# Layers' border of attention and two MLPs: last sums of two batches added by transfers and loaded back, products released before weight sums

## The chip, the core and the metric

The kernel runs on one core of one Trainium2 chip. What is measured is the device time of one execution in microseconds (us). PE is TensorE, which multiplies; DVE is VectorE, ACT is ScalarE, POOL is GpSimd; SP is SyncE, which here only issues transfers (DMAs). Each of these works through a queue of its own in order, and an instruction that waits holds up everything behind it on its queue.

## What is computed

Band attention with a few global rows gives 4 batches of 544 tokens with 512 features. They go through two MLPs ("layer 0" and "layer 1"), each with 2048 hidden columns, in float32:

```python
x = attn_out.transpose(0, 2, 1, 3).reshape(B * S, H * D)
h = x @ w_in
x = where(h > 0, h, exp(minimum(h, 0)) - 1) @ w_out         # layer 0
h = x @ w_in2
x = where(h >= 1, h, where(h <= -1, 0, (h + 1)**2 / 4)) @ w_out2   # layer 1
```

## The kernel before

A float32 number is held as two parts (high and low), and each product of two such numbers is three matmuls of 128 x 512 on PE. The 2048 hidden columns of a layer are 16 blocks `f` of 128. Two blocks make a "pair" `n`: pairs 0 to 5 are blocks 4 to 15 of layer 0, pairs 6 to 13 are all of layer 1. Four blocks, two pairs, are a "column group" `c`; two batches `j` make a "duo" (batches 0 and 1, batches 2 and 3).

**Up.** For a pair and a duo, `quad` makes eight outputs from seven products by a Strassen-like scheme: products of the weights themselves (A11, A12, A22) and of sums of weights (S1 to S4) with forms of the tokens (X11, X21, T1 and so on). `decode_in` loads a pair's raw weights into a tile named `wraw` (a pool of two tiles of 1 MB), DVE and ACT decode them into the tile `wi` (lines 213 to 239), then DVE makes the sums of weights (names `whole`, `mixed`, the last of them `wi<-mixed,wi`). `product` asks by `need` that the pair stands in `pairs_in`, which `decode_in` sets when the sums are made. `decode_out` loads and decodes the weights of the second matmul in the same way, into `wo`.

**Down.** `down` multiplies the hidden values with `wo`, over the four blocks of a column group, into four PSUM banks `dn`, one for each 128 features. `collect` takes a bank away: in most column groups ACT copies it to a tile `ev` (line 347) and a transfer issued by POOL adds it to a sum in HBM (line 352). In the last column group of a layer `so_far` holds the sum of the groups before, loaded in one transfer of 1 MB (lines 1153, 1156) while the group runs, and DVE adds the bank to it (line 355). For batches 0 and 1 that tile is one of the two `wraw` tiles; for batches 2 and 3 it is a tile `sums`.

**The border.** The layer-0 sums in `so_far` are the tokens of layer 1. `later_forms` makes their seven forms, on DVE (names `xl<-sum`, `sum<-sum`, `mixed`) and ACT (`xh<-sum`), and SP stores them for later column groups. It gets going when `summed[j]` says that the batch's last sums are issued, and it is done with a `wraw` tile only after the last form, when the next raw weights can be loaded into it.

What is written here is a program of jobs (`job_at`, `event`, `pop`): after each product a job may step and one `down` may go. From layer 0's second part on, the build's scheduler orders the instructions of each engine anew.

Of the kernel before, what the change touches and what calls it, by code (L numbers as in the profile page):

```python
# [9 lines left out]
F32 = mybir.dt.float32  # L10
# [11 lines left out]
B, H, SL, SG, D = 4, 8, 512, 32, 64  # L22
# [4 lines left out]
P = 128  # L27
# [4 lines left out]
KT = DM // P  # L32
NF = DFF // P
# [34 lines left out]
BLOCK = 2 * P  # L68
# [9 lines left out]
def band_attention_then_two_mlps(  # L78
# [40 lines left out]
    for j in range(B):  # L119
# [3 lines left out]
    so_far = {}  # L123
    dram = ctx.enter_context(tc.tile_pool(name="dram", bufs=1, space=bass.MemoryType.DRAM))

    sums = {
        (layer, j): dram.tile([P, KT, SL], F32, name=f"sum{layer}_{j}")
        for layer in range(3)
        for j in range(B)
    }  # L130
# [23 lines left out]
    eng = pinned  # L154
# [21 lines left out]
    def in_order(tag, ins):  # L176


        if eng is free:
            if tag in newest:  # L180
                tc.add_manual_dep(ins.ins, newest[tag].ins.name, IN_ORDER, reason="order of tiles")
            newest[tag] = ins

    w_in, w_out, rows_in = {}, {}, {}
# [14 lines left out]
    def decode(wtmp_p, raw, hi, lo):  # L199

        n = raw.shape[1]
        words = raw.bitcast(U32).rearrange("p (n two) -> p n two", two=2)
        low, high = words[:, :, 0], words[:, :, 1]
        top = wtmp_p.tile([P, n], U32, tag="top", name="top")
        if eng is pinned:
            power = wtmp_p.tile([P, n], U32, tag="power", name="power")
        else:
            power = raw.bitcast(U32)[:, 0:n]
        rest = wtmp_p.tile([P, n], U32, tag="rest", name="rest")
        yield  # L210

        if eng is free:
            in_order("top", eng.scalar.activation(top.bitcast(F32), high.bitcast(F32), AF.Abs))
        in_order(
            "rest",
            eng.vector.tensor_scalar(
                rest, high, 0x1FF, 15, ALU.bitwise_and, ALU.logical_shift_left
            ),
        )
        eng.vector.scalar_tensor_tensor(  # L220
            rest, low, 17, rest, ALU.logical_shift_right, ALU.bitwise_or
        )
        yield
        if eng is pinned:
            eng.scalar.activation(top.bitcast(F32), high.bitcast(F32), AF.Abs)
            yield

        eng.vector.tensor_scalar(
            top.bitcast(F32), top.bitcast(F32), SMALLEST, 1.0, ALU.max, ALU.mult
        )  # L230

        eng.vector.tensor_scalar(top, top, 3, 0x3FFFF000, ALU.logical_shift_left, ALU.bitwise_and)
        eng.vector.scalar_tensor_tensor(
            top, high, 0xC0000000, top, ALU.bitwise_and, ALU.bitwise_or
        )
        yield
        eng.scalar.activation(hi, top.bitcast(F32), AF.Copy)
        eng.vector.tensor_scalar(power, top, 0xFF800000, None, ALU.bitwise_and)
        eng.vector.scalar_tensor_tensor(
            lo, rest, 2.0 ** -35, power.bitcast(F32), ALU.mult, ALU.mult  # L240
        )
# [182 lines left out]
    def mpool(name, bufs, **kw):  # L424
        return ctx.enter_context(tc.tile_pool(name=name, bufs=bufs, reuse_waits="tile", **kw))
# [4 lines left out]
    with ExitStack() as actx:  # L430
# [413 lines left out]
        eng = free  # L844
# [5 lines left out]
    wraw_p = mpool("wraw", 2, side="right")  # L850
    wtmp_p = mpool("wtmp", 1, side="right")
    w_ps = [mpool("w_more", 1, side="right")]
# [1 line left out]
    ps_up.append(mpool("ps_up", 1, space=PSUM))  # L854
    ps_dn.append(mpool("ps_dn1", 1, space=PSUM))

    pairs_in, slot = {}, {}

    def add(out, a, b, op=ALU.add):

# [2 lines left out]
    def words(n, srcs):  # L863

        raw = wraw_p.tile([P, n * len(srcs)], U64, tag="wraw", name="wraw")
        for i, src in enumerate(srcs):
            ins = eng.sync.dma_start(raw[:, i * n:(i + 1) * n], src)
            if i == 0:
                in_order("wraw", ins)
        return raw  # L870
# [12 lines left out]
    def of_pair(n):  # L883

        layer, q = (0, n + 2) if n < 6 else (1, n - 6)
        return layer, (2 * q, 2 * q + 1)

    def decode_in(n):

        layer, fs = of_pair(n)  # L890
        raw = words(KT * P, [(w1, w2)[layer][f][:, 0:KT * P] for f in fs])
        yield
        w = w_ps[n % 3 // 2].tile([P, 2, 8 * BLOCK], F32R, tag=f"wi{n % 3}", name="wi")
        for _ in decode(wtmp_p, raw, w[:, 0, 0:4 * BLOCK], w[:, 1, 0:4 * BLOCK]):
            pass
        yield
        x = wtmp_p.tile([P, 4 * BLOCK], F32, tag="rest", name="whole")
        y = wtmp_p.tile([P, 4 * BLOCK], F32, tag="top", name="mixed")
        at = lambda t, c: t[:, c % (4 * BLOCK):c % (4 * BLOCK) + BLOCK]
        whole = add(  # L900
            x, w[:, 0, 0:4 * BLOCK].bitcast(F32), w[:, 1, 0:4 * BLOCK].bitcast(F32)
        )
        in_order("rest", whole)
        in_order("top", add(at(y, S1), at(x, A21), at(x, A22)))
        add(at(y, S2), at(y, S1), at(x, A11), ALU.subtract)
        add(at(y, S3), at(x, A11), at(x, A21), ALU.subtract)
        add(at(y, S4), at(x, A12), at(y, S2), ALU.subtract)
        hi = w[:, 0, 4 * BLOCK:]
        eng.scalar.activation(hi, y, AF.Copy)
        add(w[:, 1, 4 * BLOCK:], y, hi.bitcast(F32), ALU.subtract)  # L910
        pairs_in[n] = w
        rows_in[1, n] = lambda k, part: w[:, part, 0:4 * BLOCK].rearrange("p (f c) -> p f c", f=2)[
            :, :, k * P:(k + 1) * P
        ]

    def decode_out(n):

# [118 lines left out]
    made_forms, holds, summed, w_out_uses = set(), {}, {}, {}  # L1036
# [10 lines left out]

    def product(n, duo, col, i, then):

        need(lambda: n in pairs_in and holds.get(i) == (of_pair(n)[0], duo))  # L1050
        ps, w, x = up_bank(), pairs_in[n], slot[i]
        for k in range(2):
            for t, (a, b) in enumerate(((1, 0), (0, 1), (0, 0))):
                eng.tensor.matmul(  # L1054
                    ps,
                    w[:, a, col + k * P:col + (k + 1) * P],
                    x[b][:, k * SL:(k + 1) * SL],
                    start=k + t == 0,
                    stop=k == 1 and t == 2,
                )  # L1060
        if then is not None:

            if then + (i,) in made_forms:
                load_form(*then, i)
            else:
                holds[i] = "free"
        return ps
# [67 lines left out]
    def pop():  # L1135

        kind, *rest = downs.pop(0)
        if kind == "rows":
            _, u, layer, fs = rest
            down_rows(layer, fs, u)  # L1140
            if NF - 1 in fs:
                soon.setdefault(now[0] + 1, []).append(lambda: turn_rows(layer))
        else:
            layer, fs, j, f, ds = rest
            if f == fs[0] and len(ds) == KT:
                banks[j] = {}
            if f == fs[2 % len(fs)] and NF - 1 in fs:

                if layer == 0 and j >= 2:
                    if j == 2:  # L1150
                        spare.append(w_ps[1].tile([P, 2, 2 * BLOCK * 4], F32, tag="wi2", name="sums"))
                    so_far[layer, j] = spare[0][:, j % 2].rearrange("p (k n) -> p k n", k=KT)
                    eng.sync.dma_start(so_far[layer, j], sums[layer + 1, j])
                else:
                    so_far[layer, j] = wraw_p.tile([P, KT, SL], F32, tag="wraw", name="sum")
                    in_order("wraw", eng.sync.dma_start(so_far[layer, j], sums[layer + 1, j]))
            down(layer, fs, j, f, banks[j], ds)
            if f == fs[-1] and NF - 1 in fs and layer == 0:
                summed[j] = KT
        for f in fs if kind == "rows" else [f]:  # L1160
            if (layer, f) in pair_of:
                w_out_uses[pair_of[layer, f]] -= 1

    spare = []
    pair_of = {(of_pair(n)[0], f): n for n in range(14) for f in of_pair(n)[1]}
# [21 lines left out]
    def need(done):  # L1187

        tries = 0
        while not done():  # L1190
            step(line[0])
            tries += 1
            assert tries < 100, "what is needed is not under way"
# [26 lines left out]
    for i, js in enumerate(((0, 1, 2, 3), (2, 3, 0, 1))):  # L1220
        fs = PLAIN[i]
# [30 lines left out]
    for c in range(7):  # L1252
        at = base + 17 * c
        job_at(at + 1, decode_out(2 * c + 1))
        if c < 6:
            late = 3 if c == 3 else 0
            if c == 3:
                job_at(at + 2, later_forms(1), False)
            job_at(at + 5 + late, decode_in(2 * c + 2))
            job_at(at + 8 + late, decode_out(2 * c + 2))  # L1260
            if c == 2:
                job_at(at + 9, later_forms(0), False)
            job_at(at + 12 + late // 3, decode_in(2 * c + 3))
    for g, (c, duo) in enumerate(groups):
        n0, n1 = ns = (2 * c, 2 * c + 1)
        layer = of_pair(n0)[0]
        fs = [f for n in ns for f in of_pair(n)[1]]
# [86 lines left out]
```

## Time and profile before

| | us |
|---|---|
| median of 3 runs | 852.78 (851.49 to 853.75) |
| the profiled execution's own time | 852.66 |
| its span on the core | 850.9 |
| PE busy | 814.0 (96%) |
| DVE busy | 685.6 (81%) |
| ACT busy | 554.3 (65%) |
| POOL busy | 102.3 (12%) |

The span is the stretch from the first to the last instruction in the trace; the time has 1.8 us more around it. Matmuls overlap in the trace (one is shown with 0.39 us while they start 0.227 us apart), so PE's busy share says little; idle time in front of a matmul, and matmuls that start further apart, say more. The border of the two layers lies between 420 and 535 us.

### The profile page before, as it was taken

The page shows a single profiled execution, that of the slowest core. Times are in us where ns is not written, and L with a number is a line of the kernel's source. Part 1 is how long each engine was busy: PE and PEld are TensorE (multiplying, and loading weights), DVE is VectorE, ACT ScalarE, POOL GpSimd, SP SyncE. Part 2 cuts the span into 40 slices and gives each one's busy share as a digit, 9 for nine tenths or more (in the row PEclk, how much of TensorE's full clock was granted, in tenths as well). Part 3 has the DMA queues.
Part 4 walks back from the last instruction along what each step waited for, and adds up shares of the span by engine and source line. Part 5 has one row for each costly group of instructions (what it writes and reads, how often), then busy time and mean ns, then how long its engine had stood idle before and what let it go on. Part 6 is the DMA issues. An engine that isn't in the chain of part 4 may idle for free.

```text
span 850.9 us, 15914 instructions
## 1 busy us (share of the span) xinstructions
PE 814.0 (96%) x6058; PEld 662.6 (78%) x6058; DVE 685.6 (81%) x1279; ACT 554.3 (65%) x948; POOL 102.3 (12%) x162
## 2 busy tenths in 40 slices
PE   8799999998979999999999988999999999999998
PEld 5676778886758888888888866788888888888886
DVE  5798889968869979786789899998988598945463
ACT  5788765855746667555656366878867686867451
POOL 2231300002213022201100000000020111111000
PEclk9999999999999999999999999999999999999999
DMA  8988729997999189538916846437853795369523
GB/s 268 318 262 275 255 85 373 370 392 213 298 328 160 43 245 318 115 65 211 313 69 247 297 187 259 148 99 250 294 119 79 198 323 123 49 142 302 200 101 110
DMA packets 67132, 180.88 MB, mean 213 GB/s; under 512 B 9328, under 2 KB 9584, under 8 KB 65904
## 3 DMA queue, kind: packets, MB, share of 16 engines
q1 hardware_dynamic: 55248, 158.62, 53.8%
q0 software_dynamic: 11520, 20.98, 15.3%
q8 instruction: 48, 0.79, 0.4%
q10 hardware_dynamic: 288, 0.26, 0.1%
q14 instruction: 28, 0.23, 0.1%
HBM read 116.65 MB, written 63.18 MB: 211 GB/s over the span
## 4 chain that ended last, share of the span: by engine, by line
PE 76%; DMA 11%; DVE 7%; ACT 5%; issue 2%; POOL 0%; SPq 0%; ACTq 0%; DVEq 0%; POOLq 0%
PE dn L368 34%; PE up L1054 26%; DMA wraw<-in_w 5%; PE up L281 3%; PE dn L381 2%; DMA xh<-form 2%; PE s L146 2%; PE up L293 2%; DMA k_sb<-in_kT 1%; PE pt L146 1%; DMA sum<-ev 1%; PE up L146 1%; PE po L146 1%; ACT sn L146 1%; DVE xl L861 1%
## 5 line engine op out<-in xcount | busy, mean ns | idle before, releaser
L1054 PE MATMUL up<-xh,wi 128*128 128x512 f32 x784 | 264.5, 397 | 12.8 <-DMA xh<-form 3.9
L368 PE MATMUL dn<-gh,wo 128*128 128x512 f32 x608 | 184.6, 391 | 3.7 <-ACT ev L347 3.4
L1054 PEld LDWEIGHTS up<-xh,wi 128*128 128x128 f32 x784 | 149.9, 191 | 47.6 <-DVE u L861 4.9
L861 DVE TENSOR_TENSOR u<-up,u 128x512 f32<-128x512 f32 x196 | 131.7, 686 | 51.4 <-PE up L1054 43.2
L1054 PE MATMUL up<-xl,wi 128*128 128x512 f32 x392 | 155.0, 395 | 0.0
L352 POOL DMA_DIRECT2D sum<-ev x80 | 72.7, 1118 | 593.8 <-ACT ev L347 588.9
L368 PEld LDWEIGHTS dn<-gh,wo 128*128 128x128 f32 x608 | 113.5, 188 | 29.2 <-ACT ev L347 5.5
L368 PE MATMUL dn<-gl,wo 128*128 128x512 f32 x304 | 114.4, 390 | 0.4 <-DVE gl L334 0.4
L330 ACT ACTIVATE gh<-g 128x512 fp32r<-128x512 f32 x123 | 77.1, 628 | 53.1 <-DVE g L313 20.0
L334 DVE TENSOR_TENSOR gl<-g,gh 128x512 fp32r<-128x512 f32 x123 | 84.0, 686 | 13.0 <-ACT gh L330 11.8
L1054 PEld LDWEIGHTS up<-xl,wi 128*128 128x128 f32 x392 | 75.0, 191 | 14.9
L347 ACT ACTIVATE ev<-dn 128x512 f32<-128x512 f32 x110 | 61.7, 597 | 34.2 <-PE dn L368 19.6
L306 ACT ACTIVATE g<-u,half_sb 128x512 f32<-128x512 f32 x64 | 45.8, 720 | 48.2 <-DVE u L861 40.0
L368 PEld LDWEIGHTS dn<-gl,wo 128*128 128x128 f32 x304 | 57.0, 188 | 12.8 <-DVE gl L334 0.9
L368 PE MATMUL dn<-gh,xl 128*128 128x512 f32 x160 | 62.2, 392 | 2.6 <-ACT gh L330 2.5
L368 PE MATMUL dn<-gh,xh 128*128 128x512 f32 x160 | 62.3, 389 | 0.0
L315 DVE TENSOR_TENSOR g<-u,g 128x512 f32<-128x512 f32 x64 | 43.8, 686 | 20.9 <-ACT g L308 20.9
L368 PE MATMUL dn<-gl,xh 128*128 128x512 f32 x160 | 58.4, 389 | 0.0
L307 ACT ACTIVATE g<-g,one_sb 128x512 f32<-128x512 f32 x68 | 48.7, 720 | 1.4
L301 ACT ACTIVATE g<-u 128x512 f32<-128x512 f32 x48 | 30.1, 630 | 26.1 <-DVE u L861 22.4
L303 ACT ACTIVATE g<-g,one_sb 128x512 f32<-128x512 f32 (+1 forms) x64 | 45.6, 714 | 1.5
L308 ACT ACTIVATE g<-g 128x512 f32<-128x512 f32 x68 | 42.5, 627 | 1.1
(189 smaller groups left out, 1357.3 us busy)
## 6 DMA issues: line engine op xcount, KB each, us to landing
wraw<-in_w SPq DMA_DIRECT2D x56, 512.0 KB, 6.6
xh<-form SPq DMA_DIRECT2D x46, 512.0 KB, 9.6
xl<-form SPq DMA_DIRECT2D x46, 512.0 KB, 8.1
sum<-ev POOLq DMA_DIRECT2D x80, 256.0 KB, 8.4
v_sb<-in_vwin SPq DMA_DIRECT2D x64, 260.0 KB, 4.6
form<-xh SPq DMA_DIRECT2D x20, 512.0 KB, 4.6
form<-xl SPq DMA_DIRECT2D x20, 512.0 KB, 4.3
sum<-ev SPq DMA_DIRECT2D x32, 256.0 KB, 5.4
```

The lines of the kernel that those rows point to most:

```text
L146: return lambda *args, **kw: tc.keep_in_program_order(fn(*args, **kw))
L303: eng.scalar.activation(self.g, self.g, AF.Relu, bias=one_sb, scale=-1.0)
L306: eng.scalar.activation(self.g, self.ps, AF.Relu, bias=half_sb, scale=-0.5)
L307: eng.scalar.activation(self.g, self.g, AF.Relu, bias=one_sb, scale=-1.0)
L315: eng.vector.tensor_tensor(g, self.ps, g, ALU.max)
L330: eng.scalar.activation(self.gh, self.g, AF.Copy)
L334: eng.vector.tensor_tensor(self.gl, self.g, self.gh.bitcast(F32), ALU.subtract)
L347: eng.scalar.activation(out, ps, AF.Copy)
L352: eng.gpsimd.dma_start(to, out, accum_op=ALU.add)
L368: eng.tensor.matmul(banks[d], w[:, d * P:(d + 1) * P], g, start=first and k == 0, stop=last and k == 2)
L861: return eng.vector.tensor_tensor(out, a, b, op)
L1054: eng.tensor.matmul(ps, w[:, a, col + k * P:col + (k + 1) * P], x[b][:, k * SL:(k + 1) * SL], start=k + t == 0, stop=k == 1 and t == 2,)
```

## The change

1. In layer 0's last column group, batches 0 and 2 (the first of each duo) no longer add on DVE. Their `so_far` is not set while `down` runs, so `collect` copies each bank on ACT and adds it to the sum in HBM by a transfer of POOL's. When the batch's last `down` is issued, `all_so_far` loads the finished sum in one transfer, and `summed` is set.
2. `pairs_in[n]` is set as soon as a pair's weights are decoded; a new set `sums_in` is filled when the sums of weights are made. A product of the weights themselves asks for the first, a product of sums for the second.
3. In the first column group of layer 1 (c = 3), two of the weight jobs come one event later (`late` 4 for 3).

```diff
-    pairs_in, slot = {}, {}
+    pairs_in, sums_in, slot = {}, set(), {}
...
         for _ in decode(wtmp_p, raw, w[:, 0, 0:4 * BLOCK], w[:, 1, 0:4 * BLOCK]):
             pass
+        pairs_in[n] = w
+        rows_in[1, n] = lambda k, part: ...
         yield
...
         add(w[:, 1, 4 * BLOCK:], y, hi.bitcast(F32), ALU.subtract)
-        pairs_in[n] = w
-        rows_in[1, n] = lambda k, part: ...
+        sums_in.add(n)
...
-        need(lambda: n in pairs_in and holds.get(i) == (of_pair(n)[0], duo))
+        there = pairs_in if col < 4 * BLOCK else sums_in
+        need(lambda: n in there and holds.get(i) == (of_pair(n)[0], duo))
...
-            if f == fs[2 % len(fs)] and NF - 1 in fs:
-
-                if layer == 0 and j >= 2:
-                    if j == 2:
-                        spare.append(w_ps[1].tile([P, 2, 2 * BLOCK * 4], F32, tag="wi2", name="sums"))
-                    so_far[layer, j] = spare[0][:, j % 2].rearrange("p (k n) -> p k n", k=KT)
-                    eng.sync.dma_start(so_far[layer, j], sums[layer + 1, j])
-                else:
-                    so_far[layer, j] = wraw_p.tile([P, KT, SL], F32, tag="wraw", name="sum")
-                    in_order("wraw", eng.sync.dma_start(so_far[layer, j], sums[layer + 1, j]))
+            by_hand = NF - 1 in fs and (layer == 1 or j % 2)
+            if by_hand and f == fs[2 % len(fs)]:
+
+                all_so_far(layer, j)
             down(layer, fs, j, f, banks[j], ds)
             if f == fs[-1] and NF - 1 in fs and layer == 0:
+                if not by_hand:
+                    all_so_far(layer, j)
                 summed[j] = KT
...
-            late = 3 if c == 3 else 0
+            late = 4 if c == 3 else 0
```

`all_so_far` holds the removed lines as a function. The scheduler moves much around the border, of which three places matter below.

**SP's queue ahead of layer 1's first weights.** `sum1_0` and `sum1_1` are the sums of batches 0 and 1 in HBM, `wraw` from `in_w2` are raw weights of layer 1 (here those of `decode_out` for pair 6), `form0` are token forms. Before (the load of `sum1_0` stands six rows above these):

```order
L1027 DMA xh_5577<-form0_1_3_125 128x1024
L867 DMA wraw_5724<-in_w2 128x512 x2
L1027 DMA xl_5600<-form0_1_5_127 128x1024
L1027 DMA xh_5599<-form0_1_5_127 128x1024
L1027 DMA xl_5644<-form0_1_6_128 128x1024
L1027 DMA xh_5643<-form0_1_6_128 128x1024
L1156 DMA sum_5853<-sum1_1_108 128x2048
```

Now:

```order
L1028 DMA xl_5600<-form0_1_5_127 128x1024
L1028 DMA xh_5599<-form0_1_5_127 128x1024
L1028 DMA xl_5644<-form0_1_6_128 128x1024
L1028 DMA xh_5643<-form0_1_6_128 128x1024
L1171 DMA sum_5730<-sum1_0_107 128x2048
L867 DMA wraw_5732<-in_w2 128x512 x2
L1171 DMA sum_5861<-sum1_1_108 128x2048
```

The load of batch 0's sum has moved behind the last token forms, and the raw weights have moved behind it.

**DVE's queue in the last column group of layer 0.** `L216` begins the decoding of those raw weights, `L355` are adds of batch 0 and `u<-up` sums of products. Before:

```order
L861 TENSOR_TENSOR wi_5624<-mixed_5671,wi_5624 128x1024
L216 TENSOR_SCALAR rest_5780<-wraw_5724 128x1024
L334 TENSOR_TENSOR gl_5610<-g_5604,gh_5608 128x512
L313 SCALAR_TENSOR_TENSOR g_5648<-u_5393,g_5648 128x512
L220 SCALAR_TENSOR_TENSOR rest_5780<-wraw_5724,rest_5780 128x1024
L228 TENSOR_SCALAR top_5779<-top_5779 128x1024
L334 TENSOR_TENSOR gl_5654<-g_5648,gh_5652 128x512
L232 TENSOR_SCALAR top_5779<-top_5779 128x1024
L313 SCALAR_TENSOR_TENSOR g_5704<-up_5679,g_5704 128x512
L355 TENSOR_TENSOR sum_5656<-dn_5551,sum_5656 128x512
```

Now, ten rows after the same `wi<-mixed,wi`:

```order
L861 TENSOR_TENSOR u_5813<-up_5806,u_5742 128x512
L216 TENSOR_SCALAR rest_5788<-wraw_5732 128x1024
L861 TENSOR_TENSOR u_5834<-up_5827,u_5813 128x512
L220 SCALAR_TENSOR_TENSOR rest_5788<-wraw_5732,rest_5788 128x1024
L861 TENSOR_TENSOR u_5742<-up_5827,u_5742 128x512
L228 TENSOR_SCALAR top_5787<-top_5787 128x1024
L861 TENSOR_TENSOR u_5813<-up_5845,u_5813 128x512
L313 SCALAR_TENSOR_TENSOR g_5837<-u_5834,g_5837 128x512
L232 TENSOR_SCALAR top_5787<-top_5787 128x1024
L233 SCALAR_TENSOR_TENSOR top_5787<-wraw_5732,top_5787 128x1024
```

The decoding now begins ten instructions later, among the sums of products. The four adds of batch 0 are gone; those of batch 1 (`L355 sum_5861<-dn_5761` and three more) stand 22 instructions behind this `L216` row.

**ACT's queue at the first evictions of layer 1.** `ev<-dn` empties the banks of layer 1's first batch, `L237` makes the high part of decoded weights. Before:

```order
L306 ACTIVATE g_6521<-up_6496,half_sb_71 128x512
L308 ACTIVATE g_6469<-g_6469 128x512
L347 ACTIVATE ev_6529<-dn_6385 128x512
L347 ACTIVATE ev_6535<-dn_6389 128x512
L347 ACTIVATE ev_6541<-dn_6393 128x512
L307 ACTIVATE g_6521<-g_6521,one_sb_72 128x512
L347 ACTIVATE ev_6547<-dn_6397 128x512
L237 ACTIVATE wi_6605<-top_6606 128x1024
```

Now:

```order
L306 ACTIVATE g_6537<-up_6512,half_sb_71 128x512
L308 ACTIVATE g_6485<-g_6485 128x512
L307 ACTIVATE g_6537<-g_6537,one_sb_72 128x512
L237 ACTIVATE wi_6650<-top_6651 128x1024
L308 ACTIVATE g_6537<-g_6537 128x512
L347 ACTIVATE ev_6545<-dn_6401 128x512
L347 ACTIVATE ev_6551<-dn_6405 128x512
```

The evictions have moved behind the high part of the next pair's weights.

## Rows read from the trace of the kernel before

**Rows 1.** Windows: us, PE, PEld, DVE, ACT, POOL busy, PEclk, DMA share, GB/s.
```profile
483.00:535.00 52.00, 43.36 (x183) 33.94 (x182) 51.08 (x66) 33.40 (x49) 0.00 (x0) 0.93 0.58 215
535.00:560.00 25.00, 25.00 (x113) 20.67 (x113) 23.47 (x35) 19.92 (x31) 0.00 (x0) 1.00 0.49 152
...
500.00:505.00 5.00, 4.19 (x12) 3.26 (x13) 5.00 (x7) 1.91 (x3) 0.00 (x0) 0.68 0.27 107
```

**Rows 2.** Chain of waits that ended last, at 395 us: start, us, what.
```profile
395.15 2.72 PE up L1054 x12
```

**Rows 3.** Timeline of PE: start, us, instruction, in brackets idle before and releaser.
```profile
422.34 1.55 PE L368 MATMUL dn<-gh,wo 128*128 128x512 f32 x6
424.33 0.97 PE L368 MATMUL dn<-gl,wo 128*128 128x512 f32 x3 [0.44 <-DVE gl L334]
...
425.82 0.40 PE L1054 MATMUL up<-xh,wi 128*128 128x512 f32 x1
...
496.21 0.50 PE L1054 MATMUL up<-xh,wi 128*128 128x512 f32 x1 [0.83 <-DVE u L861]
...
500.81 0.50 PE L1054 MATMUL up<-xh,wi 128*128 128x512 f32 x1 [2.95 <-DVE wi L861]
...
514.23 0.50 PE L1054 MATMUL up<-xh,wi 128*128 128x512 f32 x1 [1.80 <-DVE u L861]
...
529.45 0.50 PE L368 MATMUL dn<-gh,xl 128*128 128x512 f32 x1 [1.98 <-ACT gh L330]
...
533.09 0.73 PE L368 MATMUL dn<-gh,wo 128*128 128x512 f32 x2 [0.63 <-ACT ev L347]
```

**Rows 4.** Timeline of DVE, 422 to 530 us, same columns.
```profile
422.98 0.69 DVE L216 TENSOR_SCALAR rest<-wraw 128x1024 uint32<-128x1024 uint32 x1 [3.61 <-DMA wraw<-in_w]
...
428.34 1.88 DVE L355 TENSOR_TENSOR sum<-dn,sum 128x512 f32<-128x512 f32 x3
430.13 1.21 DVE L233 SCALAR_TENSOR_TENSOR top<-wraw,top 128x1024 uint32<-128x1024 uint32 x1
431.27 0.68 DVE L355 TENSOR_TENSOR sum<-dn,sum 128x512 f32<-128x512 f32 x1
...
483.43 0.69 DVE L216 TENSOR_SCALAR rest<-wraw 128x1024 uint32<-128x1024 uint32 x1 [1.68 <-DMA wraw<-in_w]
...
488.73 1.23 DVE L239 SCALAR_TENSOR_TENSOR wi<-rest,wraw 128x1024 fp32r<-128x1024 uint32 x1
...
499.54 1.22 DVE L861 TENSOR_TENSOR wi<-mixed,wi 128x1024 fp32r<-128x1024 f32 x1
...
528.04 0.69 DVE L315 TENSOR_TENSOR g<-u,g 128x512 f32<-128x512 f32 x1
```

**Rows 5.** Transfers of line 352, windows 250 to 260 and 404 to 409 us.
```profile
L352 POOL DMA_DIRECT2D sum<-ev x4: 865/1140/1305, 255.1 to 258.3; - x4
...
DMA to landing us min/median/max: 4.9/6.7/6.9
...
L352 POOL DMA_DIRECT2D sum<-ev x4: 865/865/980, 404.9 to 407.8; - x4
...
DMA to landing us min/median/max: 8.0/10.0/12.4
```

**Rows 6.** Loads of 1 MB: line 1156 at 435 us, 1153 at 463, 867 at 490.
```profile
DMA to landing us min/median/max: 4.7/4.7/4.7
...
L1153 SPq DMA_DIRECT2D sums<-sum x2: 319/504/690, 463.2 to 463.6; - x2
...
DMA to landing us min/median/max: 6.5/8.0/9.6
...
DMA to landing us min/median/max: 5.6/6.0/6.4
```

**Rows 7.** Timeline of POOL, 202 to 409 us.
```profile
202.55 4.45 POOL L352 DMA_DIRECT2D sum<-ev  x4 [94.76 <-ACT ev L347]
...
404.92 2.76 POOL L352 DMA_DIRECT2D sum<-ev  x3 [17.58 <-ACT ev L347]
```

More of the change, by code (lines that the diff above doesn't have):

```diff
@@ L895, in decode_in @@
             pass
+        pairs_in[n] = w
+        rows_in[1, n] = lambda k, part: w[:, part, 0:4 * BLOCK].rearrange("p (f c) -> p f c", f=2)[
+            :, :, k * P:(k + 1) * P
+        ]
         yield
@@ L910, in decode_in @@
         add(w[:, 1, 4 * BLOCK:], y, hi.bitcast(F32), ALU.subtract)
-        pairs_in[n] = w
-        rows_in[1, n] = lambda k, part: w[:, part, 0:4 * BLOCK].rearrange("p (f c) -> p f c", f=2)[
-            :, :, k * P:(k + 1) * P
-        ]
+        sums_in.add(n)
     def decode_out(n):
@@ L1162, in pop, with all_so_far @@
                 w_out_uses[pair_of[layer, f]] -= 1
+    def all_so_far(layer, j):
+        if layer == 0 and j >= 2:
+            if j == 2:
+                spare.append(w_ps[1].tile([P, 2, 2 * BLOCK * 4], F32, tag="wi2", name="sums"))
+            so_far[layer, j] = spare[0][:, j % 2].rearrange("p (k n) -> p k n", k=KT)
+            eng.sync.dma_start(so_far[layer, j], sums[layer + 1, j])
+        else:
+            so_far[layer, j] = wraw_p.tile([P, KT, SL], F32, tag="wraw", name="sum")
+            in_order("wraw", eng.sync.dma_start(so_far[layer, j], sums[layer + 1, j]))
     spare = []
```

## Prediction

> **What bounds the kernel now.** I read the windows first, then PE's timeline, then DVE's. PE issues a 128 x 512 matmul every 0.227 us when nothing holds it: 12 take 2.72 us [rows 2]. From 535 us it has no idle time [rows 1]. The border is the exception: between 483 and 535 us PE is busy 43.4 of 52 us, while DVE is busy 51.1 [rows 1]. DVE bounds that stretch, and PE waits for it by name. Counting from start to start, less 0.23 us for a matmul, PE loses there [rows 3]: 1.0 us before 496.2 (idle 0.83, and the slower resume), 3.1 before 500.8 (2.95; the sums of weights, `wi`, are late), 2.0 before 514.2 (1.80), 2.1 before 529.5 (1.98, `gh` is late because DVE's `g` is) and 0.8 before 533.1 (0.63, an eviction). After the wait of 2.95 the granted clock falls: its mean is 0.68 over 500 to 505 us [rows 1], so the lower level, 1.2 GHz, was granted for about two thirds of that stretch; against the upper level, 2.4 GHz, it costs 5 x 0.32 = 1.6 us. All this, at least 10.6 us, is what a better border can give back, and nothing else is idle enough to matter.
>
> DVE's own stretch starts late because it waits 1.68 us for raw weights at 483.4 [rows 4].
>
> **What the change takes away.** Eight adds of DVE go. On a busy DVE an add of 512 columns costs the distance to the next start: 428.34 to 430.13 for three, so 0.60 each, 4.8 us in all; an operation of 1024 columns with two tensors costs 1.14 (430.13 to 431.27) [rows 4]. ACT copies eight banks more, which I cost at nothing where they stand: ACT is busy 33 of 52 us in the border [rows 1]; without that cover they would cost about what the adds did. The decoding that stood ahead of batch 0's last low parts goes too: DVE waits 3.61 us for its raw weights [rows 4], and PE gets its operand late, 0.44 us idle and, from start to start over the group, **0.6 us lost** [rows 3]. That wait disappears.
>
> **What it adds: a queue on SP.** The load of batch 0's sum now waits on SP until four adding transfers have landed, and the raw weights are behind it on SP. PE does batch 0's last down from 422.3 to 425.8 [rows 3], 0.6 earlier at its end now; the first bank is done after three matmuls, an eviction takes about 0.6, so POOL issues the first transfer near 423.9. Four such transfers in a quiet stretch were issued from 255.1 to 258.3 and the slowest took 6.9: all landed within 10 us of the first issue; in a loaded stretch 404.9 to 407.8 and 12.4, so 15.3 [rows 5]. I take 10, since after 424 us the loads of token forms are over: SP goes on at 434. A sum of 1 MB takes 4.7 us alone; of two in a row the second landed 3.5 us after the first (463.6 + 9.6 against 463.2 + 6.5) [rows 6]. So the raw weights land at 434 + 4.7 + 3.5, plus 0.2 for SP's issues: **442.4**. Bounds: 441 (6.4 us for weights alone [rows 6], after 434.5) and 447.5 (transfers of 15.3 us).
>
> DVE gets to the first decoding instruction after the product ahead of it. By the order PE issues 43 matmuls from batch 0's end (425.2) to there, four of them small: 434.6, DVE is there at 435.2. It then stands idle **7.2 us**. Behind it on DVE are 22 instructions up to the first add of batch 1, 17 at 0.60 and 5 at 1.14: 15.9 us, so that add ends at 442.4 + 15.9 + 0.6 = 458.9 and frees the bank that batch 2 needs. (Batch 1's sum, which needs the decoded tile's place, is issued near 452 and is there at 457.) PE comes to that bank after 130 matmuls: 425.2 + 29.0 = 454.2, plus some 1.4 for two up-banks that are copied late behind the same decoding: 455.6. It waits 3.3. So 1.4 + 3.3 = **4.7 us** of new waits. A wait of 2.95 made the clock fall [rows 1, 3]; this one should, for **1.6** more.
>
> **Lateness carried to the border.** PE comes there 4.7 + 1.6 - 0.6 = 5.7 late. The raw weights of pair 7 do not delay it: DVE frees their place about 7 us later than before, but SP has one load of 1 MB less ahead of them, and they land near 482, as before. What is late now is DVE's first add of batch 3, which stands behind the first decoding instruction and waits for PE: PE's product before it, and a 0.4 us wait for the evicted bank, put it at 484.6. The decoding ends 7.5 us later, at 492.1, where before it ended at 489.96 (488.73 + 1.23) [rows 4]: DVE is 2.1 late.
>
> For PE the lateness is first given back: the sums of weights end at about 501.6 (before 500.76 [rows 4]; in the new order the first forms of batch 2 stand behind them), and PE arrives at 501.8. The waits of 1.0 and 3.1 and their clock, 1.6, are not paid: **-5.7**, and PE is level at 505 us. From there DVE's queue holds the same instructions as before, without idle time, so its `g` that ended at 528.73 [rows 4] ends 2.1 to 2.4 later, and PE's waits grow by as much: **+2.3**. Last, the evictions of layer 1's first batch now stand on ACT behind the high part of the next weights, which waits for decoding on DVE: the wait of 0.8 before 533.1 becomes about 2.1, **+1.3**. After that PE was never idle [rows 1] and I count no change; the later weight jobs (`late`) leave DVE less to do before 545 us, which nothing waits for.
>
> The second part, products without sums, I cost at nothing: at the border the first product of sums still stands between the same products, and nothing moves on PE ahead of 422 us.
>
> **Sum** against the profiled execution's 852.66 us (0.1 below the median of the runs, 852.78): -0.6 + 4.7 + 1.6 - 5.7 + 2.3 + 1.3 = +3.6, so **856.2 us**.
>
> **Rivals.**
> - *Faster.* DVE's idle time is free until the raw weights land at about 439: then batch 1's first add ends at 455.5, PE waits next to nothing and its clock stays up. The 4.8 us of adds are then a gain: DVE's forms end earlier, pair 7's weights, with 1 MB less ahead of them, land 3.1 us earlier (9.6 against 6.5 [rows 6]), DVE starts its stretch earlier and every PE wait from 495 on shrinks. -0.6 - 3.1: **849.0 us**. For it: DVE waits for those weights at 483 [rows 4]. Against it: each of the three landings in a row would have to beat the shortest row I have.
> - *No difference.* The raw weights land at 441: PE's new waits are 4.7 - 1.4 = 3.3, the last of them too short for the clock to fall, and PE comes 2.7 late. DVE is then level with before at 490; PE's 2.7 is given back whole in its waits at 495 to 501, and only the eviction's 1.3 is left: **853.9 us**. For it: a chain of three landings was taken at near its shortest rows already, and 1.4 us less decides. Against it: three landings rarely all come at their shortest.
> - *Slower still.* POOL's four transfers take 15.3 us, as in the loaded stretch [rows 5]: the weights land at 447.5, PE's wait and DVE's lateness grow by 5.1: **861.3 us**. Batch 2's sum, behind the same kind of transfers, would be loaded from 497.3 to 502.0, just when DVE wants its forms (502.3): 0.8 more at most. For it: the transfers' landing is the widest of my rows. Another way there is that DVE's decoding holds POOL up. Four issues beside a whole decoding took POOL 4.45 us; three beside mostly plain operations took 2.76, or 3.7 for four [rows 7]: 0.8 us of difference, and no decoding stands beside batch 0's four issues in the new order. The Trainium skill (SBUF — State Buffer, "SBUF: two separate sides") says that a DMA issued from POOL cannot get its descriptors written while DVE runs an operation in a two-port mode; by that rule each of the four issues of batch 2 could wait out a decoding operation of 0.69, which would add an estimated 2.8 us to its load. The rows bear out less than a third of that.
> - *It does not do what it says*: releasing products before the sums would have spared 3.1 + 1.6 us at 500; in the new order the wait goes only because PE comes late. This is inside the forecast.
>
> **How the numbers follow.** A difference under 0.3% (2.6 us) is about what a measurement of this kernel can't tell from none. The forecast has 0.42 and slower still 0.14: slower 0.56. No difference 0.24. Faster 0.20. The slower cases reach from 855.4 to 861.3, as the landing moves from 441 to 447.5. The range takes in these, the 853.9 and the faster rival's 849.0, with half a us beyond that one for the spread of the runs: 848.5 to 861.5.
>
> **What would show it.** Right: SP issues batch 0's sum near 434 and the raw weights behind it land near 442; DVE's L216 shows about 7 us idle "<-DMA wraw"; PE waits about 3 us for an add (L355) near 455 to 459, with a lower clock behind it; the 2.95 wait for `wi` is gone; waits at 512 to 534 are longer. Wrong: that idle time under 3 us, or PE without a wait before 470; then the border decides, and the faster rival holds. If PE waits there and the time still falls, my carrying of lateness through DVE's queue is wrong.

## The result and the profile after

The changed kernel took 864.88 us (median of 4 runs, 863.63 to 867.0) beside 852.13 for the kernel before on the same chip: a ratio of 1.015, 95% interval 1.0124 to 1.0177. A second series gave 1.0111 (1.008 to 1.0141). It is slower by 9 to 13 us, where the forecast was 3.6 and the range ended at 861.5. The direction was right, the size was not.

The profiled execution took 864.94 us, its span is 863.2 us, 12.3 more than before. Where this comes from can be counted on PE, start to start, as in the prediction. I set the zero at the first of the 24 small matmuls of line 293 that stand just ahead of the change's first difference on PE (419.47 us before, 421.36 after). What lies ahead of it is the same in both kernels, and over the fourteen profiled executions of this study it ended anywhere between 418.29 and 424.38: **1.9 of the 12.3 us are that scatter**. The other 10.4 come in two nearly equal parts:

| PE loses, us | before | after | more | forecast |
|---|---|---|---|---|
| the next 60.5 us (to the border) | 1.2 | 6.4 | 5.2 | 5.7 |
| the 80 us after that (the border) | 13.3 | 18.6 | 5.2 | -2.1 |
| the rest | 0.6 | 0.5 | 0 | 0 |

The first row went as forecast, the second went the other way. Windows after (us, busy of PE, PEld, DVE, ACT, POOL, then PEclk, DMA share, GB/s), to be read against [rows 1]:

```profile
453.00:464.00 11.00, 7.87 (x22) 5.28 (x21) 10.37 (x16) 5.04 (x8) 0.00 (x0) 0.69 0.80 276
483.00:535.00 52.00, 43.40 (x189) 33.90 (x188) 45.09 (x60) 29.97 (x44) 3.54 (x4) 0.97 0.78 257
535.00:560.00 25.00, 21.93 (x86) 17.13 (x85) 24.68 (x36) 20.40 (x32) 0.00 (x0) 0.86 0.44 159
500.00:505.00 5.00, 3.75 (x17) 2.65 (x15) 4.93 (x10) 1.66 (x2) 0.00 (x0) 1.00 0.96 304
```

In the border DVE is busy 45.1 us of 52, where it was 51.1: it stood idle, most of it in the waits shown next (batch 2's adds, which are gone, stood ahead of 483 us). The DMA engines were busy for 0.78 of the stretch instead of 0.58. After 535 us, where PE had no idle time before, it now lacks 3 us.

What holds DVE up stands in its timeline (start, us, instruction, in brackets idle time before and what ended it), against [rows 4]:

```profile
443.44 0.69 DVE L216 TENSOR_SCALAR rest<-wraw 128x1024 uint32<-128x1024 uint32 x1 [6.23 <-DMA wraw<-in_w]
...
460.30 2.48 DVE L355 TENSOR_TENSOR sum<-dn,sum 128x512 f32<-128x512 f32 x4 [0.63 <-DMA sum<-sum]
...
490.63 0.69 DVE L216 TENSOR_SCALAR rest<-wraw 128x1024 uint32<-128x1024 uint32 x1 [5.13 <-DMA wraw<-in_w]
...
497.37 1.23 DVE L239 SCALAR_TENSOR_TENSOR wi<-rest,wraw 128x1024 fp32r<-128x1024 uint32 x1
...
509.68 2.36 DVE L861 TENSOR_TENSOR xl<-sums,xh 128x1024 fp32r<-128x1024 f32 x2 [1.11 <-ACT xh L952]
```

Two waits for raw weights, of 6.23 and 5.13 us, where there were 3.61 and 1.68. The first belongs to the decoding that now stands behind batch 0's sum, the second to pair 7.

POOL issued the first of batch 0's transfers at 426.02, and SP's timeline shows where those weights were issued:

```profile
426.02 0.86 POOL L352 DMA_DIRECT2D sum<-ev  x1 [15.42 <-ACT ev L347]
...
435.85 0.32 SPq L1171 DMA_DIRECT2D sum<-sum  x1
436.27 0.84 SPq L867 DMA_DIRECT2D wraw<-in_w  x2
453.87 0.33 SPq L1171 DMA_DIRECT2D sum<-sum  x1
...
477.28 1.16 SPq L867 DMA_DIRECT2D wraw<-in_w  x2
...
501.01 0.33 SPq L1168 DMA_DIRECT2D sums<-sum  x1
```

and the time from issue to landing of pair 7's load is, after (issued at 477.28) and before (issued at 468.39):

```profile
L867 SPq DMA_DIRECT2D wraw<-in_w x2: 333/554/774, 477.3 to 477.7; - x2
...
DMA to landing us min/median/max: 11.2/12.0/12.9
```

```profile
L867 SPq DMA_DIRECT2D wraw<-in_w x2: 332/582/833, 468.4 to 468.8; - x2
...
DMA to landing us min/median/max: 13.5/14.0/14.6
```

So pair 7's weights were issued 8.9 us later (7.0 without the scatter), needed 1.7 us less, and landed at 490.5, not 483.3. While they were under way the DMA engines were full (share 1.02 in the window row):

```profile
477.00:490.50 13.50, 13.23 (x59) 10.62 (x58) 6.55 (x10) 5.87 (x10) 3.54 (x4) 1.00 1.02 331
```

The last row of SP above is the load of batch 2's sum. It lands at 508.57, and ACT, whose forms of batch 2 go ahead of DVE's, waits 4.43 us for it:

```profile
508.59 2.00 ACT L952 ACTIVATE xh<-sums 128x1024 fp32r<-128x1024 f32 x2 [4.43 <-DMA sums<-sum]
```

PE's waits over 0.3 us, against [rows 3]:

```profile
455.65 0.50 PE L1056 MATMUL up<-xh,wi 128*128 128x512 f32 x1 [2.17 <-DVE u L861]
...
458.52 0.79 PE L1056 MATMUL up<-xh,wi 128*128 128x512 f32 x1 [0.95 <-DVE u L861]
...
498.65 0.50 PE L1056 MATMUL up<-xh,wi 128*128 128x512 f32 x1 [0.34 <-DVE wi L239]
...
506.90 0.51 PE L1056 MATMUL up<-xh,wi 128*128 128x512 f32 x1 [3.15 <-DVE u L861]
...
521.60 0.47 PE L1056 MATMUL up<-xh,wi 128*128 128x512 f32 x1 [1.68 <-DVE u L861]
...
524.19 0.50 PE L1056 MATMUL up<-xh,wi 128*128 128x512 f32 x1 [0.99 <-ACT u L1086]
...
529.65 0.50 PE L368 MATMUL dn<-gh,xl 128*128 128x512 f32 x1 [1.88 <-DVE xl L239]
...
539.60 0.80 PE L368 MATMUL dn<-gh,xl 128*128 128x512 f32 x1 [2.86 <-ACT gh L330]
```

Behind the waits at 458, 507 and 539 us matmuls start 0.427 us apart instead of 0.227 for 3 to 6 us: the lower clock was granted there (a mean of 0.69 over 453 to 464 and of 0.86 over 535 to 560 in the windows above).

### The profile page after: what moved, and what is told of

Read it like the earlier page. It is cut to its first block, busy times and chain, and to the rows that moved or that the text cites. A ratio compares the mean times of both kernels' runs of the same rounds, so it can differ in the third digit from the quotient of the medians.

```text
span 863.2 us, 15940 instructions
## 1 busy us (share of the span) xinstructions
PE 819.8 (95%) x6058; PEld 666.3 (77%) x6058; DVE 682.8 (79%) x1271; ACT 559.0 (65%) x956; POOL 109.5 (13%) x170
## 4 chain that ended last, share of the span: by engine, by line
PE 61%; issue 16%; DVE 9%; DMA 7%; ACT 3%; POOL 2%; SPq 0%; POOLq 0%; ACTq 0%; DVEq 0%
PE dn L368 27%; PE up L1056 19%; PE up L281 3%; DMA sum<-ev 2%; DMA xh<-form 2%; POOL sum L352 2%; PE dn L381 2%; PE s L146 2%; PE up L146 1%; PE up L293 1%; PE pt L146 1%; DVE u L861 1%; PE po L146 1%; DMA sums<-sum 1%; DMA k_sb<-in_kT 1%
## 5 line engine op out<-in xcount | busy, mean ns | idle before, releaser
L352 POOL DMA_DIRECT2D sum<-ev x88 | 81.5, 1207 | 596.6 <-ACT ev L347 591.9
L347 ACT ACTIVATE ev<-dn 128x512 f32<-128x512 f32 x118 | 65.6, 596 | 31.9 <-PE dn L368 19.1
L368 PE MATMUL dn<-gh,xl 128*128 128x512 f32 x160 | 64.3, 404 | 5.5 <-ACT gh L330 3.4
L368 PE MATMUL dn<-gl,xh 128*128 128x512 f32 x160 | 60.8, 398 | 0.0
L213 ACT ACTIVATE top<-wraw 128x1024 f32<-128x1024 f32 x29 | 33.3, 1150 | 23.8 <-DMA wraw<-in_w 13.2
```

Of the source, the lines that this page charges most:

```text
L347: eng.scalar.activation(out, ps, AF.Copy)
L352: eng.gpsimd.dma_start(to, out, accum_op=ALU.add)
L368: eng.tensor.matmul(banks[d], w[:, d * P:(d + 1) * P], g, start=first and k == 0, stop=last and k == 2)
```

## The experiments

My theory after reading the two traces was **two causes**: batch 0's sum, waited for on SP, holds up the raw weights of pair 6 and with them all that follows; and batch 2's adding transfers fill the DMA engines at the border. The rivals were **one cause** (only the first matters, the border follows from it) and **only batch 2**. All runs side by side; "PE loses" is counted as above, in the 60.5 us and the 80 us after the zero:

| run | ratio to before (95%) | PE loses |
|---|---|---|
| kernel before | 1 | 1.2 / 13.3 |
| changed, first series | 1.015 (1.0124 to 1.0177) | 6.4 / 18.6 |
| changed again | 1.0111 (1.008 to 1.0141) | 6.2 / 16.9 |
| second part only | 1.0003 (0.998 to 1.0025) | 1.2 / 12.5 |
| batch 0 only | 1.0081 (1.0056 to 1.0106) | 6.1 / 15.4 |
| batch 2 only | 1.0002 (0.998 to 1.0025) | 0.7 / 13.3 |
| changed, sum loaded from POOL | 0.9999 (0.9975 to 1.0022) | 0.8 / 13.2 |
| batch 0 only, sum loaded from POOL | 0.9992 (0.9976 to 1.0007) | 0.9 / 14.0 |
| changed, batch 2 without adding | 1.0107 (1.0072 to 1.0142) | 6.7 / 17.2 |
| batch 3 only | 1.0036 (1.0015 to 1.0057) | 0.8 / 17.6 |
| two loads from POOL | 1.0059 (1.0034 to 1.0083) | 0.7 / 18.4 |
| sum from POOL, weights first | 1.0027 (1.0008 to 1.0047) | 0.8 / 15.4 |
| before, weights first | 0.9999 (0.9981 to 1.0017) | 0.8 / 14.7 |
| batch 2 only, weights first | 1.0024 (1.0006 to 1.0042) | 1.0 / 15.2 |

**The change once more.** 

> The changed kernel once more, unedited, beside the other runs on the same chip, so that they can be compared with it: 862 to 867, the loss on PE between 424 and 480 us again 6 to 7 us, after 480 us again about 18.

863.51 us, PE's losses 6.2 and 16.9. The first part repeats in size, though not in kind: the full clock was granted here, and all of the loss is waits, one of them for an add of batch 1.

```profile
453.00:464.00 11.00, 6.70 (x27) 4.62 (x26) 10.23 (x16) 4.76 (x7) 0.00 (x0) 1.00 0.84 275
```

```profile
461.00 0.47 PE L368 MATMUL dn<-gh,xl 128*128 128x512 f32 x1 [1.09 <-DVE sum L355]
```

The border's part differs by 1.7 us between two executions of one kernel, so a difference of that size in single traces says little.

**The second part alone.**

```diff
-            by_hand = NF - 1 in fs and (layer == 1 or j % 2)
+            by_hand = NF - 1 in fs
```

> Only the second part and the later weight jobs: products without sums, late = 4; all four batches still add on DVE. All theories: the order on PE is that of the kernel before, so the same time within 2 us of it (850.5 to 854.5), with the wait of about 3 us for wi near 498 still there. If it is over 855, part of the loss belongs to the later weight jobs, which I counted as nothing.

854.36 beside 853.99 us. PE's order is that of the kernel before, and products released earlier and later weight jobs change nothing, as they were priced. The wait for the sums of weights, which the early release was to spare, stands as it was (2.95 [rows 3]):

```profile
501.60 0.79 PE L1056 MATMUL up<-xh,wi 128*128 128x512 f32 x1 [2.95 <-DVE wi L861]
```

**Batch 0 alone.**

```diff
-            by_hand = NF - 1 in fs and (layer == 1 or j % 2)
+            by_hand = NF - 1 in fs and (layer == 1 or j != 0)
```

> Batch 0 by adding transfers, batch 2 by DVE again. Two causes (SP's queue delays the raw weights, and batch 2's adding transfers fill the DMA engines at the border): the wait of DVE L216 for about 6 us near 437 and PE's 6.4 us of loss near 453 to 463 stay, the border loses about what it lost before; 856 to 860. One cause (everything follows from the first delay): as the changed kernel, 863 to 866. Only batch 2 matters: 851 to 854.

861.33 us, 7.3 more than before, which itself stood at 853.99 in this series, 1.9 above the first. By itself 861.33 lies between what two causes said (856 to 860) and what one cause said (863 to 866); with the 1.9 taken off it is 859.4, the upper end of two causes. DVE's timeline:

```profile
443.09 0.69 DVE L216 TENSOR_SCALAR rest<-wraw 128x1024 uint32<-128x1024 uint32 x1 [5.98 <-DMA wraw<-in_w]
...
491.59 0.70 DVE L216 TENSOR_SCALAR rest<-wraw 128x1024 uint32<-128x1024 uint32 x1 [1.39 <-DMA wraw<-in_w]
```

The wait of 6 us is there, and pair 7's weights are as late as in the changed kernel (491.5) without any transfer of batch 2. DVE's wait for them is short because DVE, which has batch 2's adds here, comes to them only at 490.2; in the changed kernel it stood idle from 485.5.

**Batch 2 alone.**

```diff
-            by_hand = NF - 1 in fs and (layer == 1 or j % 2)
+            by_hand = NF - 1 in fs and (layer == 1 or j != 2)
```

> Batch 2 by adding transfers, batch 0 by DVE. Two causes: no wait near 437 nor 453; the four adding transfers still take 1.5 to 1.9 us each of a full DMA stretch, raw weights of pair 7 or batch 2's sum land late, 854 to 858. One cause: the same as before or up to 3 us faster for the four adds saved, 849 to 853. Only batch 2 matters: 862 to 866.

854.22 us, no change. "Only batch 2" is out. DVE's timeline:

```profile
480.63 0.69 DVE L216 TENSOR_SCALAR rest<-wraw 128x1024 uint32<-128x1024 uint32 x1 [4.68 <-DMA wraw<-in_w]
...
498.74 2.35 DVE L861 TENSOR_TENSOR xl<-sums,xh 128x1024 fp32r<-128x1024 f32 x2
```

The kernel before has 1.68 for this wait [rows 4], and this for the first forms of batch 2:

```profile
496.67 2.36 DVE L861 TENSOR_TENSOR xl<-sums,xh 128x1024 fp32r<-128x1024 f32 x2
```

The four adds saved stand ahead of DVE's wait for pair 7's weights, and the wait grew by 3.0 us. Counted from the zero, the weights landed 2.6 us earlier, with one sum less ahead of them, and the sums of weights ended 2.3 us earlier; but batch 2's forms begin 2.3 us later, since its sum now comes through HBM (ACT waits 2.94 us for it). PE's loss in the border is 13.3 us, as before.

**The changed kernel with batch 0's sum on another queue.** Both parts of the change and all eight adding transfers stay.

```diff
-            in_order("wraw", eng.sync.dma_start(so_far[layer, j], sums[layer + 1, j]))
+            load = eng.gpsimd if (layer, j) == (0, 0) else eng.sync
+            in_order("wraw", load.dma_start(so_far[layer, j], sums[layer + 1, j]))
```

> The changed kernel, but batch 0's sum is loaded from POOL's queue, so that SP's loads of raw weights do not wait behind it. Two causes: the raw weights land before 432, DVE L216 does not wait for them, PE's 6.4 us at 453 to 463 are gone, what is left is the collision at the border: 854 to 858. One cause: 849 to 853. Only batch 2: 862 to 866. If the wait moves to the load of the sum itself, DVE waits for sum near 452 instead.

854.03 us, ratio 0.9999. The weights are issued at 419.25 and landed at 428.1; DVE reaches them without a wait, and waits for pair 7's like this:

```profile
435.49 0.69 DVE L216 TENSOR_SCALAR rest<-wraw 128x1024 uint32<-128x1024 uint32 x1
...
482.10 0.69 DVE L216 TENSOR_SCALAR rest<-wraw 128x1024 uint32<-128x1024 uint32 x1 [3.10 <-DMA wraw<-in_w]
...
500.55 2.36 DVE L861 TENSOR_TENSOR xl<-sums,xh 128x1024 fp32r<-128x1024 f32 x2 [0.52 <-ACT xh L952]
```

Over 453 to 464 us PE has no idle time and the full clock:

```profile
453.00:464.00 11.00, 11.00 (x50) 9.09 (x50) 11.00 (x15) 5.51 (x7) 0.00 (x0) 1.00 0.54 215
```

The whole loss of the change is gone, the border's part too (13.2 us, before 13.3), though batch 2's transfers are still there. Taken as a number, 854.03 is the lower end of "two causes" and 1 us above "one cause"; but the kernel before stood at 853.99 beside it, so nothing is left for a second cause. The adds saved gave nothing back.

**Batch 0 alone, its sum on another queue** (the same edit on the run with batch 0 alone).

> Batch 0 alone by adding transfers, as in the run that was 7 us slower, but its sum is loaded from POOL's queue; batch 2 adds on DVE. If SP's queue is the whole of that run's loss: DVE's wait of 6 us near 437 and PE's 6 us at 453 to 463 are gone, PE loses 12 to 14 us after 480, and the time is that of the kernel before within 1 us. If the four adds saved, which stand where DVE has time, count after all: 1 to 2.5 us faster. If something else of batch 0's transfers delays the border (the later evictions, their time on the DMA engines): 3 us or more slower than before.

853.56 us, 0.9992 (0.9976 to 1.0007), against 1.0081 with the load on SP. Between these two runs only the queue of one load differs, and with it the scheduler's order: 7.6 us. What the new order does by itself no run separates. POOL issues the load no earlier than SP did, 15.4 us after the zero where SP took 14.3 with batch 0 alone:

```profile
435.12 0.57 POOL L1172 DMA_DIRECT2D sum<-sum  x1 [7.03 <-DVE rest L216]
```

So the sum is no earlier; what is gained is that no weights wait behind it. The four adds saved show no gain.

**Batch 2's transfers without the adding.**

```diff
-                eng.gpsimd.dma_start(to, out, accum_op=ALU.add)
+                if layer == 0 and j == 2 and NF - 1 in fs:
+                    eng.gpsimd.dma_start(to, out)
+                else:
+                    eng.gpsimd.dma_start(to, out, accum_op=ALU.add)
```

> The changed kernel, but batch 2's four transfers store the bank instead of adding it, so that their sum lacks the column groups before; everything else stays. If the adding transfers' time on the DMA engines (some 1.5 us each, against 0.6 for a plain one of that size) is what batch 2 costs at the border, batch 2's sum is loaded about 3 us earlier than at 501 and PE loses 2 to 4 us less after 480 us: 861 to 863. If it is only that the load waits at all, or nothing of batch 2: 864 to 866.

863.34 us beside 863.51 for the changed kernel on the same chip: no difference, a miss for the second cause as I had stated it. Batch 2's sum was issued 1.0 us earlier, counted from the zero (78.4 against 79.4 us), not 3. The DMA engines did feel it. The queue of POOL's transfers over 482 to 502 us, adding (the changed kernel again) and storing (columns: packets, MB, share of 16 engines):

```profile
q0 software_dynamic: 576, 1.05, 30.0%
```

```profile
q0 software_dynamic: 320, 1.05, 16.6%
```

That is 6.0 against 3.3 us of all sixteen engines for the same bytes, but pair 7's weights landed 69.3 us after the zero where the changed kernel had 69.2 and 67.2 in its two profiles: no earlier, and the end did not move.

**Batch 3 alone.**

```diff
-            by_hand = NF - 1 in fs and (layer == 1 or j % 2)
+            by_hand = NF - 1 in fs and (layer == 1 or j != 3)
```

> Batch 3 alone by adding transfers, the others on DVE. The adds of batches 0 and 2 stand ahead of DVE's wait for pair 7's raw weights, those of batch 3 behind it. If adds count only behind that wait, 2.4 us of DVE's queue are saved where it bounds PE: PE's loss after 480 us falls from 13.3 to 11 or 12, the time is 1 to 2.5 us below the kernel before. If batch 3's sum comes too late for its forms (DVE wants it near 512): 855 to 860. If adds count wherever they stand: no better than batch 2 alone, within 1 us of the kernel before.

858.23 us, 3.9 slower: the second case. DVE's sums of weights were done at 492.9, with the scatter taken off 6.7 us earlier than the 500.76 of before, and then

```profile
505.29 1.23 DVE L861 TENSOR_TENSOR sums<-sums 128x1024 f32<-128x1024 f32 x1 [5.36 <-DMA sums<-sum]
```

DVE waits 5.36 us for batch 3's sum. Of the 6.7 us, 2.9 are weights of pair 7 that landed earlier, four adds are worth 2.4 at most, and the scheduler's order has changed too; so what the adds alone give where DVE bounds PE, this run does not show. The way through HBM is longer than the time that is left.

**Two loads from POOL's queue.** As the run with the sum on POOL's queue, and:

```diff
-    def words(n, srcs):
+    def words(n, srcs, queue=None):
...
-            ins = eng.sync.dma_start(raw[:, i * n:(i + 1) * n], src)
+            ins = (queue or eng.sync).dma_start(raw[:, i * n:(i + 1) * n], src)
...
-        raw = words(KT * P, [(w1, w2)[layer][f][:, 0:KT * P] for f in fs])
+        raw = words(KT * P, [(w1, w2)[layer][f][:, 0:KT * P] for f in fs], eng.gpsimd if n == 7 else None)
```

> The changed kernel with batch 0's sum loaded from POOL's queue, and pair 7's raw weights too, so that they do not stand behind the forms' stores on SP. If the wait for those weights is what swallows the adds saved, they land 3 us or more earlier than 482, DVE's wait there goes, and the whole gains 1.5 to 3.5 us over the kernel before. If the DMA engines are simply full there, they land as late as before and the time is that of the kernel before within 1 us.

859.42 us. Pair 7's weights were issued at 471.3 and 471.9 and landed at 482.3; from SP's queue, in the run before that, they were issued at 470.6 and 470.9 and landed at 482.1. The second case, as far as the landing goes: the issue was no earlier, and the DMA engines are full there, whatever queue feeds them (share 1.03 over 471 to 482.3 here, 1.02 over 470.5 to 482.1 there). By the Trainium skill (DMA: Bandwidth & Descriptors, "Issuing engines are not separate DMA queues") transfers from different issuing engines run on the same 16 DMA engines and interleave; these two landings agree. The 5 us lost on top I did not settle: the scheduler ordered DVE anew, and pair 7's last sum of weights starts at 505.19 instead of 498.22.

**Pair 7's weights ahead of batch 3's sum.** The scheduler is given an order: the load of batch 3's sum behind the weights' load, the next weights and the later stores behind that sum.

```diff
+            if j == 3:
+                tc.add_manual_dep(ins.ins, weights_7[0].ins.name, IN_ORDER, reason="behind the weights")
+                sum_3.append(ins)
...
+            if sum_3:
+                tc.add_manual_dep(ins.ins, sum_3[0].ins.name, IN_ORDER, reason="behind the sum")
```

With batch 0's sum on POOL's queue: 

> Batch 0's sum loaded from POOL's queue, as before, and the load of batch 3's sum (1 MB) put behind pair 7's raw weights on SP instead of ahead of them. If those weights' landing sets DVE's border, they land 2 to 3 us before the 482 of the run with the load on POOL alone, DVE's wait of 3.1 us there shrinks by as much, PE loses 1.5 to 2.5 us less after 480 us: 1.5 to 3 us below the kernel before. If batch 3's sum is then what DVE waits for, DVE shows a wait for it behind the decoding and the time is that of the kernel before or above. If the landing does not matter: within 1 us of the kernel before with the earlier landing all the same.

856.18 us, 2 slower than before, a miss. The weights landed at 479.35, 2.7 us earlier, as expected, and the timelines of DVE and ACT show

```profile
479.44 0.69 DVE L216 TENSOR_SCALAR rest<-wraw 128x1024 uint32<-128x1024 uint32 x1 [2.17 <-DMA wraw<-in_w]
...
499.31 2.01 ACT L958 ACTIVATE xh<-sums 128x1024 fp32r<-128x1024 f32 x2 [2.32 <-DMA sums<-sum]
500.40 1.22 DVE L862 TENSOR_TENSOR xl<-sums,xh 128x1024 fp32r<-128x1024 f32 x1 [1.19 <-ACT xh L958]
```

DVE came to the weights earlier too, so the wait only fell from 3.10 to 2.17; and batch 2's forms still begin at 500.4, with the scatter taken off 2.0 us later than before. They wait for batch 2's sum, on ACT. The weights' landing is not what alone sets the border.

On the kernel with all adds on DVE: 

> All adds on DVE as in the kernel before, and batch 3's sum loaded behind pair 7's raw weights (and, by the scheduler, behind the next ones). DVE waits 1.7 us for those weights in the kernel before, and they would land 2.6 us earlier: at most 1.7 us faster. The sum's load stands behind another 1 MB here, so that DVE may wait for it near 488 instead: then 854 to 858.

853.99 us, 0.9999. DVE's wait for the weights stays (1.75) and one of 1.25 for the sum comes on top.

On the kernel with batch 2 alone: 

> Batch 2 alone by adding transfers, and batch 3's sum loaded behind the raw weights of pair 7 and the next 1 MB. DVE's wait of 4.7 us for pair 7's weights shrinks by 2 to 3 us; the sum lands near 490, when DVE wants it from 484 on: what is gained at the weights is lost at the sum, within 1.5 us of the kernel before. If the weights' landing alone decides: 2 to 3 us below it.

856.56 us, 1.0024: the sum is waited for (2.25 us at 490.45), and the run is 2.3 us slower where I had allowed 1.5: a miss.

No run was faster than the kernel before by more than its interval.

## Why the prediction was wrong

- **What bounds the kernel**: right. Nothing outside 420 to 560 us changed but the scatter ahead of it.
- **The queue on SP**: right, and borne out by the two runs that move this one load to another queue (the scheduler's order changes with it). The first of batch 0's transfers was issued at 426.0 (forecast 423.9, plus 1.9 of scatter), SP went on 9.8 us later (forecast 10), the weights landed 7.5 us after that (8.4), DVE stood idle 6.23 us (7.2).
- **New waits on PE, 4.7 + 1.6 - 0.6 = 5.7**: right in size, 5.2, and wrong in name. Batch 1's first add ended at 460.98, and I had 458.9, or 460.8 with the scatter; but PE waited mostly for copies of up-banks behind the same decoding, 2.17 and 0.95, and the bank of the add was a wait of its own (1.09) only in the second profile. That the parts add up to nearly the forecast is luck in part: in the first profile the lower clock cost 2.6 us where I had 1.6, in the second it was not granted at all and the waits were longer.
- **"They land near 482, as before"** is the step that failed. The weights of pair 7 were issued 7 us later, net of scatter, just as I had it. But I let them land as before, which leaves them 6.6 us, the time of a load with little ahead of it [rows 6]. They stood behind a sum and five stores of forms issued in the 5 us before them and took 11.2 to 12.9, where behind two sums and four stores they had taken 13.5 to 14.6: one load of 1 MB less ahead of them saved 1.7 us, not 7. The forms' stores are late by the same cause as the weights (batch 1's sum is loaded at 453.87 instead of 434.95, since it needs the place of pair 6's raw weights, whose decoding ends at 453.80), so the crowd on the DMA engines moved along with them. In the run with batch 0 alone, without batch 2's transfers, they were as late (491.5). That the late landing carries the loss into the border is read from the trace (DVE's wait of 5.13 us): no run changes that landing alone in the changed kernel.
- **The lateness given back, -5.7**: fell with it; in the first 32 us of the border PE lost 6.3 us (4.6 in the second profile) where it had lost 6.0 before, so the term measured +0.3. I had DVE's decoding end at 492.1, 494.0 with the scatter; it ended at 498.6. The waits before 501 shrank to 0.34, as forecast, but one of 3.15 with a lower clock stands at 503.8 to 506.9 in their place.
- **The later waits, +2.3 and +1.3**: they grew by 4.9 instead of 3.6, from a DVE 6.7 us late at the end of that decoding (scatter taken off) instead of 2.1. The mechanisms that I named show in part: in the first profile the wait for `gh` was 2.86 with the lower clock behind it and that for an eviction 0.21, in the second 1.25 and 2.70. With the step above the border came to +5.2 instead of -2.1.
- **Batch 2's transfers.** I charged them 0.8 at most, in a rival, with the sum loaded from 497.3 to 502.0. In the changed kernel the four took up to 15.3 us to land, and the sum was loaded from 499.1 to 506.7 with the scatter taken off; ACT waited for it, and batch 2's forms began 3.1 and 4.9 us later, counted from the zero, than in the run with batch 0 alone. Alone they cost nothing (1.0002), and with batch 0's sum off SP nothing either (0.9999). Beside the late weights PE loses 16.9 to 18.6 us in the border with them and 15.4 without: 1.5 to 3.2 more in single traces, of the size of their scatter. It is not the adding (run without it). What of this is batch 2's is not settled.
- **The adds taken off DVE** I had counted as no gain of their own, and that holds. Batch 0's stood where PE does not wait for DVE; batch 2's stood ahead of a wait that grew by more than they were worth, and what DVE won there was lost at batch 2's later forms.
- **Second part at nothing**: right, 1.0003.
- **Readings of the trace before.** I counted one stretch at the lower clock, behind 500 us. There is a second one, behind the wait of 1.80 before 514.2 [rows 3] and one of 0.45 after it, so PE lost 13.3 us in the border and not only the 10.6 that I listed:

```profile
515.00:520.00 5.00, 4.55 (x14) 3.13 (x13) 5.00 (x7) 1.56 (x3) 0.00 (x0) 0.66 0.55 217
```

So "too short for the clock to fall", said of a wait of some 1.9 us in the rival "no difference", was no safe reading. And with weights landing at 441 that rival has 853.9 while my slower cases begin with 441 at 855.4: the two do not fit together.
- **The rivals.** "Slower still" was at 861.3, by late transfers; those came at 10 us, so its mechanism was not the one. That a late start at the border makes the DMA backlog late as well, and so costs at both ends, was in none of my cases; the seventh of the chance that I had put near the measured time stood on another cause. The second half of "faster" was met by the run with the sum on POOL's queue: pair 7's weights landed 2.9 us earlier and DVE's sums of weights ended 3.0 us earlier, counted from the zero. PE's waits did not shrink for it (13.2 us); batch 2's forms began 2.2 us later.

## What to carry to other kernels

A load that has to wait for a chain of transfers should not stand on the queue that also feeds the decoding: put it on a queue with nothing behind it, and the same edit costs nothing instead of 1%. When a stall delays a producer, the transfers that it feeds move along and meet the next load as before: do not take a load's landing as fixed, nor price it from a quiet stretch, before listing what is issued in the 10 us ahead of it. Work taken off an engine ahead of its next wait was no gain here: the wait grew by as much and more.

## What the runs showed of the hardware that I had not expected

- Four adding transfers of 256 KB took the time of all 16 DMA engines for 6.0 us, four that only store the same tiles 3.3 us (30.0% and 16.6% of 20 us).
- A load issued by POOL landed as one issued by SP did: batch 0's sum 5.2 us after POOL's issue at 437.0, against 4.7 from SP, and pair 7's weights within 0.2 us of each other.
- The stretch ahead of the change, the same instructions in all kernels, ended between 418.29 and 424.38 us. A single profile thus can't tell differences of 2 us unless they are counted from a common instruction.
